# Windowed attention into a two-layer MLP: q/k loads moved to the end of the batch before, eight groups of 256 tokens, buffer fills on POOL and DVE

## The chip, the cores and the metric

One core of one Trainium2 chip. The metric is the device time of the kernel in microseconds (us), the median of several runs. Engines: PE (TensorE, matmuls; its weight loads are listed as PEld), DVE (VectorE), ACT (ScalarE), POOL (GpSimd) and SP (SyncE, which here only issues DMAs, in the order of the program). Every engine works through its own queue in order and waits for others by semaphores.

## The reference

q, k and v are 8 batches x 8 heads x 576 tokens x 64, fp32. Attention is limited to a window of 32 tokens on either side. Its output, with the heads side by side, is a matrix of 4608 tokens x 512, and goes through two matrices with a leaky ReLU between them.

```python
scores = scale * np.matmul(q, k.transpose(0, 1, 3, 2))
mask = np.abs(pos[:, None] - pos[None, :]) <= window
scores = np.where(mask, scores, -1000000000.0)
attn = np.exp(scores - max); attn = attn / sum(attn)
x = np.matmul(attn, v)                      # 4608 x 512 in all
h = x @ w_in                                # 512 x 2048
out = np.maximum(0.01 * h, h) @ w_out       # 2048 x 512
```

## The kernel before

**Attention** goes in steps of one pair of heads each. Batches 0 and 1 (`BY_DMA = 2`, steps 0 to 15, "old" steps) are done in half batches of 288 tokens; their queries and keys are transposed on PE (`transposes`, L321). Batches 2 to 7 (steps 16 to 71) are done in blocks of 64 tokens, four blocks and one pair of heads to a step; their queries and keys are transposed by DMA (`transpose_dma`, L302). A step of the new kind is:
- `score_blocks` (L370): four matmuls of 128 columns (L377), an exponential on ACT (L382), a product with the band mask on POOL (L384). It runs two steps ahead.
- `product_blocks` (L388): eight matmuls of 64 columns (L395) that give the weighted values and, through columns of ones beside the values, the sums; two ACT copies (L402, L403), a reciprocal (L404) and two products into `xT` (L408) on DVE.

**The MLP** goes in groups of tokens (`GROUPS`, L490). For each of 16 tiles f of the hidden layer `h_tile` issues four matmuls (L500) into one of four PSUM buffers `mm`, and ACT applies the leaky ReLU into `gT` (L514). Then `o_tile` (L537) makes 128 tokens of output from 16 matmuls of 512 columns (L549), ACT copies them (L554), and SP stores them (L555, three buffers `o_sb`). The groups are four of 288 tokens (batches 0 and 1), four of 256, four of 512 and one of 384.

**Order.** Up to group 1 the order is written out by hand (L625 to L748). From there a plan of "h" and "o" units with a cost each (L753 to L762) runs on a clock, and each attention step has a due time (L768 to L779) such that every group has its tokens 5 us ahead; `spend` (L783) puts a step before the first unit whose clock has reached its due time. `step` (L585) issues the scores of step i + 2, the weighted values of step i, the copies of transposed queries into their padded buffer on DVE (`place_queries`, L314 to L319), then what is due for later batches, and last one `chore`.

**Preparing a batch b.** `base(b)` is its first step: 16, 24, 32 (b = 2 to 4), 40, 52, 60. At step `base(b) + p - 7` POOL casts q and k of pair p (`cast_qk`, L285), and SP issues their two transposes (L305), which wait for the casts. Three steps later DVE places the queries, one step after that (`base(b) + p - 3`) POOL casts v (`cast_vw`, L298 to L300). q and k of one pair index have one buffer (`qf`, `kf`), v too (`vbuf`), so a load of batch b + 1 waits for the cast of batch b. Before the change, `load_qk(b + 1, p)` (L82, L87) stands in the step of `cast_qk(b, p)`, behind its transposes; batch 3 is loaded in steps 13 to 16, batch 2 by `second_pair` (L723). `load_v_pairs` (L109, five DMAs for two pairs) of the next batch stands at step `base(b) + p - 2` with p = 1 and 3.

**Fills.** The new steps need two sets of buffers `qz` (queries, zero in the other head's rows), `kz` and `vw` (values, with columns of ones). They share memory with the buffers of batches 0 and 1 and are filled while these are worked on, by generators that do one fill each time they are asked: `clear_q` (L228; ACT at L233, others at L236), `set_ones` (L239; ACT at L244, others at L249, each with two small POOL fills), `clear_k` (L254). The list `chores` is worked off by `chore()`, the list `more` by `chore(more)`. Before the change, ACT fills six parts of `qz` at tiles f = 4 to 9 of group 0 while DVE fills six others at f = 5, 7, ... 15; at f = 8 to 15 of group 1 DVE clears the last four parts and sets the first two ones; ACT sets the other six ones at steps 14, 15 and 17 to 20. POOL also clears `kbd[1]` and `vbd[1]` of batch 1 (L719, L746).

Of the kernel before, what the change touches and what calls it, by code (L numbers as in the profile page):

```python
# [16 lines left out]
def kernel(  # L17
# [15 lines left out]
    nc = tc.nc  # L33

    B, H, S, D = q.shape
# [5 lines left out]
    NPAIR = H // 2  # L41
# [25 lines left out]
    BY_DMA = 2  # L67

    def load_qk(b, p, behind=None):

        for into, src, name in ((qf, q, "qf"), (kf, k, "kf")):
            t = fload.tile([96, 2, RUN * D], FP32, name=f"{name}{p}")
            if behind is not None:
                behind.memset(t[0:1, 0, 0:1], 0.0)
                behind = None
            heads = src[b, 2 * p:2 * p + 2]
            if b < BY_DMA:
                nc.sync.dma_start(out=t, in_=heads.rearrange("a (p c) d -> p a (c d)", c=RUN))  # L80
            elif into is qf:
                nc.sync.dma_start(  # L82
                    out=t.rearrange("p a (g e) -> p a g e", g=3),
                    in_=heads.rearrange("a (g p c) d -> p a g (c d)", g=3, c=2),
                )
            else:
                nc.sync.dma_start(  # L87
                    out=t.rearrange("p a (c d) -> p a c d", d=D),
                    in_=heads.rearrange("a (c p) d -> p a c d", p=96),
                )  # L90
            into[b, p] = t
# [96 lines left out]
    for lo in (0, 64):  # L188
# [3 lines left out]
            base=0, channel_multiplier=-1, pattern=[[1, 2], [0, 3], [2, 64]],  # L192
# [3 lines left out]
            base=2 * W, channel_multiplier=1, pattern=[[-1, 2], [0, 3], [-2, 64]],  # L196
# [31 lines left out]
    def clear_q(i, pairs, eng):  # L228
        for p in pairs:
            for a in range(2):  # L230
                r = slice(64 * (1 - a), 64 * (1 - a) + 64)
                if eng is nc.scalar:
                    eng.activation(  # L233
                        out=qz[i][r, p, a], in_=zero[r].to_broadcast([64, S]), func=AF.Copy)
                else:
                    eng.memset(qz[i][r, p, a], 0.0)  # L236
                yield

    def set_ones(i, pairs, eng):  # L239

        for p in pairs:
            to = vw[i][:, p, :, 1]
            if eng is nc.scalar:
                eng.activation(  # L244
                    out=to, in_=one.to_broadcast([128, NB * D]).rearrange("p (m d) -> p m d", d=D),
                    func=AF.Copy,
                )
            else:
                eng.memset(to, 1.0)  # L249
            nc.gpsimd.memset(vw[i][0:W, p, 0, 1], 0.0)  # L250
            nc.gpsimd.memset(vw[i][128 - W:128, p, NB - 1, 1], 0.0)
            yield

    def clear_k(i):  # L254
        nc.gpsimd.memset(kz[i][:, :, 0:W], 0.0)
        nc.gpsimd.memset(kz[i][:, :, KPAD - W:], 0.0)
        yield
# [21 lines left out]
    def cast_qk(b, p, q_eng=None):  # L279
        for eng, src, dst in ((q_eng or nc.gpsimd, qf, qb), (nc.gpsimd, kf, kb)):  # L280
            to, tok = dst[:, p], src[b, p].rearrange("p a (c d) -> p c a d", d=D)
            if eng is nc.scalar:
                eng.activation(out=to, in_=tok, func=AF.Copy)
            else:
                eng.tensor_copy(out=to, in_=tok)  # L285
# [25 lines left out]
    def base(b):  # L311
        return OLD + NPAIR * (NB * (b - BY_DMA) // 4)

    def place_queries():  # L314
        while landing and landing[0][0] <= state["done"]:
            _, b, p, t = landing.pop(0)
            for a in range(2):
                r = slice(64 * a, 64 * a + 64)
                nc.vector.tensor_copy(out=qz[b % 2][r, p, a], in_=t[r])  # L319
# [30 lines left out]
    def place_keys():  # L350

        while unplaced:
            b, p, kT = unplaced.pop(0)
            for a in range(2):
                r = slice(64 * a, 64 * a + 64)
                nc.vector.tensor_copy(  # L356
                    out=kbd[b % 2][r, p, :, r], in_=kT[r].rearrange("p (n j) -> p n j", j=64))
# [52 lines left out]
    def score(i):  # L410
        if i >= OLD:
            return score_blocks(i)
        b, hf, p = where(i)
        by_c = qT[b][:, p].rearrange("p (c i) -> p c i", c=2)
        for n_, blocks in enumerate(WIN[hf]):
            for blk, i0, n in blocks:
                nc.tensor.matmul(  # L417
                    ps_v[:, n_, :, i0:i0 + n], kbd[b % 2][:, p, blk],
                    by_c[:, :, hf * EVEN + i0:hf * EVEN + i0 + n], start=True, stop=True,
                )  # L420
        e = attn.tile([128, 2 * HALF], BF16, name="e")
        nc.scalar.activation(out=e, in_=ps[:, P0:P0 + 2 * HALF], func=AF.Exp, scale=scale)  # L422
        pr = prob[:, i % NPROB]
        nc.gpsimd.tensor_mul(  # L424
            pr.rearrange("p n c i -> p (n c i)"), e, mask[hf].rearrange("p n c i -> p (n c i)"),
        )
        probs[i] = [pr, None, None]

    def join(i):


        pr = probs[i][0].rearrange("p n c i -> p n (c i)")
        both = joined.tile([128, HALF], BF16, name="both")
        nc.vector.tensor_add(both, pr[:, 0], pr[:, 1])
        probs[i][1] = both
# [42 lines left out]
    def weighted(i):  # L478
        if i >= OLD:
            return product_blocks(i)  # L480
        if probs[i][2] is None:
            sums(i)
        product(i)
        scaled(i)
# [5 lines left out]
    GROUPS = [(HALF * g, HALF) for g in range(2 * BY_DMA)]  # L490
    t0, new = 0, NTOK - BY_DMA * S
    while t0 < new:
        n = 256 if t0 < 1024 else min(512, new - t0)
        GROUPS.append((t0 % NEW_RING, n))
        t0 += n

# [71 lines left out]
    JOINED = 12  # L568
    state = {"done": 0}

    qk_due, v_due, v_next = {}, {}, {}
    for b in range(BY_DMA, B):
        for p in range(NPAIR):
            qk_due.setdefault(base(b) + p - 7, []).append((b, p))
            v_due.setdefault(base(b) + p - 3, []).append((b, p))
            if b + 1 < B and p % 2 == 1:
                v_next.setdefault(base(b) + p - 2, []).append((b + 1, p - 1))

    chores = []

    def chore(from_=chores):
        while from_ and next(from_[0], "end") == "end":
            from_.pop(0)

    def step():  # L585
        i = state["done"]
        if JOINED - 1 <= i < OLD - 1:
            join(i + 1)
        if i < NC - 2:
            score(i + 2)  # L590
        weighted(i)
        place_keys()
        place_queries()
        for b, p in qk_due.get(i, ()):
            cast_qk(b, p)
            transpose_dma(b, p)
        for b, p in v_due.get(i, ()):
            cast_vw(b, p)
        for b, p in v_next.get(i, ()):
            load_v_pairs(b, p)  # L600
        for b, p in qk_due.get(i, ()):
            if BY_DMA < b < B - 1:
                load_qk(b + 1, p)
        if 12 < i <= 12 + NPAIR:
            load_qk(BY_DMA + 1, i - 13)
        if i == OLD - 2:
            chores.append(set_ones(0, (2, 3), nc.scalar))
        if i == OLD:
            chores.extend([clear_k(1), set_ones(1, range(NPAIR), nc.scalar)])
        if OLD - 6 <= i < OLD - 3:  # L610
            next(band_parts)
        chore()
        state["done"] += 1
# [92 lines left out]
            score(i + 3)  # L706
        state["done"] += 1

    chores.extend([clear_q(1, (0, 1), nc.scalar), clear_q(0, (2,), nc.scalar)])
    more = [clear_q(1, (2, 3), nc.vector), clear_q(0, (3,), nc.vector)]  # L710
    for f in range(4, FFC):
        h_tile(0, f)
        chore()
        if f % 2 == 1:
            chore(from_=more)
        if f in (5, 9, 13):
            second_half()
        if f % 2 == 1:
            nc.gpsimd.memset((kbd if f < 12 else vbd)[1][:, (f - 4) // 2 % 4], 0.0)  # L719
    second = transposes(1)  # L720
    chores.extend([clear_q(0, (0, 1), nc.vector), clear_k(0), set_ones(0, (0, 1), nc.vector)])

    def second_pair(p):  # L723
        next(second)
# [14 lines left out]
    for f in range(4, FFC):  # L739
        h_tile(1, f)  # L740
        if f >= 8:
            chore()
        if f in (7, 11):
            second_pair((f - 7) // 4)
        if f in (7, 9):
            nc.gpsimd.memset(vbd[1][:, (f - 3) // 2], 0.0)  # L746
        if f == 13:
            score(8)  # L748
# [90 lines left out]
```

## Time and profile before

| | us |
|---|---|
| median of 3 runs | 323.22 (323.21 to 324.9) |
| the profiled execution | 323.49 |
| its span, first to last instruction | 321.8 |
| PE busy | 300.6 |
| DVE busy | 226.5 |
| ACT busy | 221.8 |
| POOL busy | 199.5 |
| granted TensorE clock, mean | 0.998 |

A group line of the profile has the source line, engine, operation, tiles written and read, shape and count, then the busy time, the mean length of one, and the engine's idle time just before them with what ended it. A timeline row has start, length, engine, line, operation, shape and count, and in brackets the idle time before it. A waits row has who waited for whom, the total in us, how often, and the longest. L numbers are lines of the kernel. "SPq" are DMA issues of SP.

The time falls into a start of some 30 us, in which loads and the first attention steps fill PE only partly, a middle up to 170 us in which all engines and the DMA queue are well used, and an end in which PE has no gap.

### The profile page before, as it was taken

To read this page: it belongs to the slowest core of one execution; us is meant where nothing else is said; L and a number is where in the kernel's file an instruction comes from. 1 tells how busy PE (TensorE), PEld (TensorE's weight loads), DVE (VectorE), ACT (ScalarE), POOL (GpSimd) and SP (SyncE) were. 2 spreads that over 40 slices of the span, in tenths; PEclk is the share of its full clock that TensorE was granted. 3 is DMA by queue.
4 is the path that set the end of the run, shared out by engine and by line. 5 is a ranking of instruction groups with operands and counts; after the bars stand their busy time and mean duration, and the time that the engine had idled before them with its cause. 6 is when DMAs were issued, how large, how long until landed. Compare 5 with 4: busy or idle time off the path is not lost.

```text
span 321.8 us, 6551 instructions
## 1 busy us (share of the span) xinstructions
PE 300.6 (93%) x2377; PEld 182.0 (57%) x2377; DVE 226.5 (70%) x295; ACT 221.8 (69%) x478; POOL 199.5 (62%) x262
## 2 busy tenths in 40 slices
PE   2778898999999989999999999999999999999995
PEld 1556674576665756767675555555555555544643
DVE  5688867879867978899799866677678766753000
ACT  7687797666795857778686975697569747852731
POOL 7888944899888867787777326677767722110000
PEclk9999999999999999999999999999999999999999
DMA  8999999977999999999989903995492011001001
GB/s 186 227 194 226 268 240 209 220 190 158 209 250 178 199 218 210 201 200 218 179 174 215 206 2 83 221 229 116 101 198 56 2 65 66 2 33 67 34 32 66
DMA packets 122416, 49.45 MB, mean 154 GB/s; under 512 B 96656, under 2 KB 117904, under 8 KB 122384
## 3 DMA queue, kind: packets, MB, share of 16 engines
q1 hardware_dynamic: 118160, 44.84, 69.4%
q0 software_dynamic: 4224, 4.19, 7.9%
q8 instruction: 18, 0.29, 0.4%
q14 instruction: 14, 0.11, 0.1%
HBM read 36.70 MB, written 9.44 MB: 143 GB/s over the span
## 4 chain that ended last, share of the span: by engine, by line
PE 79%; ACT 8%; DVE 7%; issue 2%; DMA 2%; POOL 1%; ACTq 0%; POOLq 0%; DVEq 0%
PE mm L549 35%; PE mm L500 32%; PE ps L377 4%; ACT gT L514 2%; PE s L395 2%; DMA kT<-qb 2%; PE x L395 2%; DVE set L319 2%; DVE r L451 1%; PE ps L417 1%; DVE r L404 1%; PE x L462 1%; ACT e L422 1%; DVE set L356 1%; POOL prob L424 1%
## 5 line engine op out<-in xcount | busy, mean ns | idle before, releaser
L500 PE MATMUL mm<-xT,w_in_bf 128*128 128x288 bf16 (+3 forms) x832 | 135.6, 313 | 2.5 <-ACT gT L514 2.4
L549 PE MATMUL mm<-w_out_bf,gT 128*128 128x512 bf16 (+2 forms) x592 | 131.8, 373 | 0.0
L404 DVE RECIPROCAL r<-r 128x256 f32<-128x256 f32 (+1 forms) x56 | 95.0, 1696 | 41.0 <-ACT r L403 40.4
L384 POOL TENSOR_TENSOR prob<-e,band 128x512 bf16<-128x512 bf16 (+1 forms) x56 | 62.6, 1118 | 68.1 <-ACT e L382 64.2
L500 PEld LDWEIGHTS <-w_in_bf 128*128 128x128 bf16 x832 | 79.0, 98 | 44.8 <-issue 4.2
L514 ACT ACTIVATE gT<-mm 128x288 bf16<-128x288 f32 (+3 forms) x208 | 87.9, 469 | 15.0 <-PE mm L500 11.8
L549 PEld LDWEIGHTS <-gT 128*128 128x128 bf16 x592 | 55.1, 98 | 57.7
L382 ACT ACTIVATE e<-ps 128x512 bf16<-128x512 f32 (+1 forms) x56 | 32.5, 580 | 43.5 <-PE ps L377 41.3
L554 ACT ACTIVATE o_sb<-mm 128x512 f32<-128x512 f32 (+2 forms) x37 | 21.7, 585 | 24.2 <-PE mm L549 23.6
L451 DVE RECIPROCAL r<-s 128x288 f32<-128x288 f32 x16 | 31.3, 1954 | 4.8 <-PE s L446 3.9
L285 POOL CAST kb<-kf 96x768 bf16<-96x768 f32 x32 | 27.1, 847 | 5.0 <-DMA kf<-in_k_dram 4.8
L319 DVE COPY set<-kT 64x576 bf16<-64x576 bf16 x48 | 25.3, 527 | 2.7 <-DMA kT<-qb 1.7
L408 DVE TENSOR_TENSOR xT<-s,r 64x256 bf16<-64x256 f32 (+1 forms) x56 | 23.1, 413 | 3.3
L408 DVE TENSOR_TENSOR xT<-x,r 64x256 bf16<-64x256 f32 (+1 forms) x56 | 23.1, 413 | 3.3
L424 POOL TENSOR_TENSOR prob<-e,mask 128x576 bf16<-128x576 bf16 x16 | 20.4, 1273 | 7.7 <-ACT e L422 6.7
L377 PEld LDWEIGHTS <-set 128*128 128x128 bf16 x216 | 16.9, 98 | 13.5 <-DMA set<-kb 1.6
L377 PE MATMUL ps<-set 128*128 128x128 bf16 x216 | 22.0, 219 | 2.1 <-DVE set L319 2.0
L285 POOL CAST qb<-qf 96x768 bf16<-96x768 f32 x24 | 19.7, 819 | 0.0
L298 POOL CAST set<-vbuf 128x640 bf16<-128x640 f32 x24 | 17.8, 742 | 0.7 <-DMA vbuf<-in_v_dram 0.7
L395 PEld LDWEIGHTS <-set 128*128 128x128 bf16 x432 | 18.0, 98 | 0.5
L299 POOL CAST set<-vbuf 64x512 bf16<-64x512 f32 x24 | 14.6, 610 | 1.5
L300 POOL CAST set<-vbuf 64x512 bf16<-64x512 f32 x24 | 14.6, 610 | 1.1
(74 smaller groups left out, 220.7 us busy)
## 6 DMA issues: line engine op xcount, KB each, us to landing
qf<-in_q_dram SPq DMA_DIRECT2D x32, 288.0 KB, 4.6
kf<-in_k_dram SPq DMA_DIRECT2D x32, 288.0 KB, 5.4
out_dram<-o_sb SPq DMA_DIRECT2D x35, 256.0 KB, 3.6
vbuf<-in_v_dram SPq DMA_DIRECT2D x36, 128.0 KB, 3.5
vbuf<-in_v_dram SPq DMA_DIRECT2D x16, 144.0 KB, 6.2
vbuf<-in_v_dram SPq DMA_DIRECT2D x24, 96.0 KB, 3.4
w_in_bf<-in_moe_w_in_dram POOLq DMA_DIRECT2D x4, 512.0 KB, 7.9
w_out_bf<-in_moe_w_out_dram POOLq DMA_DIRECT2D x4, 512.0 KB, 15.6
```

Of the source, the lines that this page charges most:

```text
L285: eng.tensor_copy(out=to, in_=tok)
L319: nc.vector.tensor_copy(out=qz[b % 2][r, p, a], in_=t[r])
L377: nc.tensor.matmul(sc[:, :, w], kz[b % 2][:, p, 64 * m:64 * m + 128], tok[:, :, m // 3, :, at:at + 32], start=True, stop=True,)
L382: nc.scalar.activation(out=e[:, 0:n], in_=ps[:, lo:lo + n], func=AF.Exp, scale=scale)
L384: nc.gpsimd.tensor_mul(pr, e[:, 0:n], band.rearrange("p w c i -> p (w c i)")[:, 0:n])
L395: nc.tensor.matmul(x[:, a, w], vw[b % 2][:, p, m, a:a + 2].rearrange("p n d -> p (n d)"), pr[:, a, w], start=True, stop=True,)
L404: nc.vector.reciprocal(r[:, 0:n], r[:, 0:n])
L408: nc.vector.tensor_mul(xT[rows, p, t0:t0 + n], x[rows, a], r[rows, 0:n])
L451: nc.vector.reciprocal(r, s)
L500: nc.tensor.matmul(h[:, 0:n], w_in_bf[:, c, ts(f, 128)], xT[:, c, t0:t0 + n], start=(c == 0), stop=(c == DMC - 1),)
L514: nc.scalar.activation(out=to, in_=h, func=AF.Prelu, alpha=0.01)
L549: nc.tensor.matmul(o[:, lo:hi], gT[:, f, t0:t0 + 128], w_out_bf[:, f, lo:hi], start=(f == 0), stop=(f == FFC - 1),)
```

## The change

- The loading of q and k in `step` by `qk_due` goes. A table `qk_next` puts `load_qk(b + 1, p)` at step `base(b) + p - 4`, three steps later than before and behind all four pairs of transposes of batch b. For batch 3 that is steps 12 to 15, one earlier than before.
- `load_v_pairs` of the next batch moves one step earlier, into the step of the last v cast that it waits for.
- The groups of 256 tokens go from four to eight; two of 512 go.
- The ones of set 0 (pairs 2, 3) and set 1 are set by DVE, no longer by ACT, in the same steps.
- In group 0 ACT fills nothing. DVE does six fills there as before, but of the parts that ACT had filled. The six parts that DVE had filled there are filled by POOL at f = 8 to 13 of group 1.

```diff
-        n = 256 if t0 < 1024 else min(512, new - t0)
+        n = 256 if t0 < 2048 else min(512, new - t0)
...
-    qk_due, v_due, v_next = {}, {}, {}
+    qk_due, qk_next, v_due, v_next = {}, {}, {}, {}
...
+            if b + 1 < B:
+                qk_next.setdefault(base(b) + p - 4, []).append((b + 1, p))
             if b + 1 < B and p % 2 == 1:
-                v_next.setdefault(base(b) + p - 2, []).append((b + 1, p - 1))
+                v_next.setdefault(base(b) + p - 3, []).append((b + 1, p - 1))
...
-        for b, p in qk_due.get(i, ()):
-            if BY_DMA < b < B - 1:
-                load_qk(b + 1, p)
-        if 12 < i <= 12 + NPAIR:
-            load_qk(BY_DMA + 1, i - 13)
+        for b, p in qk_next.get(i, ()):
+            load_qk(b, p)
         if i == OLD - 2:
-            chores.append(set_ones(0, (2, 3), nc.scalar))
+            chores.append(set_ones(0, (2, 3), nc.vector))
         if i == OLD:
-            chores.extend([clear_k(1), set_ones(1, range(NPAIR), nc.scalar)])
+            chores.extend([clear_k(1), set_ones(1, range(NPAIR), nc.vector)])
...
-    chores.extend([clear_q(1, (0, 1), nc.scalar), clear_q(0, (2,), nc.scalar)])
-    more = [clear_q(1, (2, 3), nc.vector), clear_q(0, (3,), nc.vector)]
+    more = [clear_q(1, (0, 1), nc.vector), clear_q(0, (2,), nc.vector)]
     for f in range(4, FFC):
         h_tile(0, f)
-        chore()
         if f % 2 == 1:
             chore(from_=more)
...
+    more = [clear_q(1, (2, 3), nc.gpsimd), clear_q(0, (3,), nc.gpsimd)]
...
         h_tile(1, f)
         if f >= 8:
             chore()
+            chore(more)
```

## The prediction

> **What bounds the kernel now.** I read the busy shares first, then the 40 slices, then the PE rows of the waits and of the timeline.
>
> ```profile
> PE 300.6 (93%) x2377; PEld 182.0 (57%) x2377; DVE 226.5 (70%) x295; ACT 221.8 (69%) x478; POOL 199.5 (62%) x262
> PE   2778898999999989999999999999999999999995
> PE mm L500 <- ACT gT L514: 2.4, 7, 0.5
> PE ps L377 <- DVE set L319: 2.0, 2, 1.3
> ```
>
> PE is the bound, and it is full from about 170 us to the end. So only PE time lost before 170 us can be won. A matmul's drawn end is modelled, so I count lost time from start to start. Runs without waits give the pitch of each shape: 216 ns for 512 columns, 122 for 288, 109 for 256. What the PE timeline has beyond these pitches is lost: 9.3 us before 30 us, 2.9 from 30 to 48.7, 1.5 to 80, 1.9 to 110, 2.4 to 140, 1.1 to 170, then nothing. The first 9.3 us lie ahead of every line that the diff touches. About 10 us are within reach, 3% of the time.
>
> ```profile
> 34.52 0.65 PE L500 MATMUL mm<-xT,w_in_bf 128*128 128x288 bf16 x4 [0.49 <-ACT gT L514]
> 34.49 0.68 ACT L233 ACTIVATE set<-zero 64x576 bf16<-64x576 bf16 x1
> 90.39 2.12 PE L500 MATMUL mm<-xT,w_in_bf 128*128 128x288 bf16 x16
> 92.89 1.14 PE L500 MATMUL mm<-xT,w_in_bf 128*128 128x288 bf16 x8 [0.37 <-ACT gT L514]
> 91.86 0.68 ACT L244 ACTIVATE set<-one 128x576 bf16<-128x576 bf16 x1
> 117.64 0.33 PE L377 MATMUL ps<-set 128*128 128x128 bf16 x3 [1.33 <-DVE set L319]
> 116.97 0.62 DVE L319 COPY set<-kT 64x576 bf16<-64x576 bf16 x2 [1.75 <-DMA kT<-qb]
> ```
>
> Columns: start, length, engine and line, [idle before, and what ended it]. Between two gT activations ACT fills a buffer for 0.68 us, and PE waits for gT. From 90.39, 16 x 122 ns end at 92.34, but PE goes on at 92.89: 0.55 lost. At 116.10 one score matmul starts, the next at 117.64: 1.48 lost, because DVE placed the queries late, because their transpose landed late.
>
> **Part 1, zero fills of the first two stretches.** Six ACT fills of 0.68 us (L233, 28.5 to 35.2) go. PE lost 0.62 + 0.51 + 0.65 = 1.78 us there. DVE does six zero fills of 0.30 us there as before, and they are late next:
>
> ```profile
> 32.06 1.95 DVE L451 RECIPROCAL r<-s 128x288 f32<-128x288 f32 x1
> 34.01 0.69 DVE L236 MEMSET set<- 64x288 uint32 x2
> 35.45 0.46 DVE L476 TENSOR_TENSOR xT<-x,r 128x288 bf16<-128x288 f32 x1 [0.74 <-PE x L462]
> ```
>
> DVE runs without a break from 26.23 to 34.70; its only slack is this 0.74. The product xT of step 7 (37.99) hangs on that chain, and group 1 needs it. So of 1.78 at most 0.74 comes through.
>
> Then POOL gets six fills at f = 8 to 13 of group 1. POOL fills cost 0.52 us for 512 elements and 1.05 for 1152, by which 576 take 0.58, together 3.5 us. They stand behind the cast at 42.68, among two 1.05 us fills:
>
> ```profile
> 43.91 2.00 DVE L285 CAST qb<-qf 96x768 bf16<-96x768 f32 x1
> 48.31 0.56 DVE L285 CAST qb<-qf 96x768 bf16<-96x768 f32 x1
> 43.45 2.05 POOL L746 MEMSET set<- 128x1152 bf16 x2
> 42.68 0.82 POOL L285 CAST kb<-kf 96x768 bf16<-96x768 f32 x1 [2.56 <-DMA kf<-in_k_dram]
> ```
>
> The same DVE cast takes 0.56 us beside an idle POOL and 2.00 beside two POOL fills; it ends 0.4 after the second. The Trainium skill (SBUF — State Buffer, Who interferes with whom) says that such a DVE cast and a POOL instruction need one port pair, which the first to issue holds for its whole length. The row agrees for one fill but not for two, since the cast stood there before the second. By that rule alone the cast would lose at most 1.05 us.
>
> POOL is idle 2.56, 1.01 and 1.93 us around the new fills, but the second gap waits for a load (kf, landing at 46.5), so not all of it is usable. The key cast at 46.50 moves to some 48 or 49, the first prob product behind it from 49.96 to about 50.9. PE needs that product near 52. Best case: the DVE cast, due 0.74 earlier at 43.2, gets in right after the cast at 42.68, ends at 44.0 in place of 45.9, and the 0.60 us that PE lost at 47.5 (score, L417, waiting for L356) goes as well: +1.3. Worst case: it waits for all 2 x 1.05 + 4 x 0.58 = 4.4 us of fills: -2.3, below. I take **+0.5**, nearer to the good end, since a cast on POOL did let a DVE cast in at 38.3.
>
> **Part 2, ones of the second buffers (L244 to L249).** ACT loses six times 0.68 us. PE lost 0.54 + 0.55 in group 3, each right behind such a fill. The group before, without a fill in it (and with lighter steps on ACT), lost nothing. **+1.0**. DVE gains six times 0.54 (the L249 row). At steps 17 to 19 DVE idles 1.2 to 1.7 us before each reciprocal, which covers it; at 14 and 15 it is dense, but PE has the wider spacing of part 4. At step 20 it is not covered, which part 3 counts.
>
> **Part 3, the loads.** Line 603 issued two DMAs (0.57 + 0.51 us of SP) right behind each pair of transposes. Now they come three steps later, behind all four pairs. The v loads (five DMAs, 3.2 to 4.9 us of SP) move one step earlier, ahead of the next batch's transposes.
>
> ```profile
> 109.28 0.57 SPq L82 DMA_DIRECT2D qf<-in_q_dram  x1
> 109.90 0.50 SPq L87 DMA_DIRECT2D kf<-in_k_dram  x1
> 110.50 0.54 SPq L555 DMA_DIRECT2D out_dram<-o_sb  x1
> 111.14 1.32 SPq L305 DMA_TRANSPOSE kT<-qb  x1
> ```
>
> POOL had cast this pair by 101.9; SP reached its transpose at 111.14, and it landed at 116.94. Without three pairs of loads (3.3 us) and the v loads at 96.12 (3.9) ahead of it, it lands before DVE is free at 115.2. Lost around there: 0.80 (108.66) + 0.23 + 1.48 = 2.51. What is late next is DVE: reciprocal 1.75, two products 0.86, two copies 1.5, and once 0.54 for the ones. The step spacing helps: from step 20 to step 23 PE has 10.0 us of work before, 10.9 after. The first loss becomes 0.80 + 0.54 - 0.88 = 0.46, the others nothing: **+2.0** (from 0.9, if DVE gains nothing from the spacing, to 2.5). The next batch lost 0.16 + 0.25 in the same way: **+0.2**.
>
> New waits: the v load now waits on SP for POOL's three casts of its own step (1.9 us). Behind it stand output stores, which have three buffers, the next q/k loads, needed five or more steps (18 us) later, and transposes that need a later POOL cast anyway. Batch 3's loads go one step earlier, ahead of batch 2's last v load (some 1.1 us of SP): its cast waited 0.70 at 82.05 already, but the prob product behind it is ready 4.4 us ahead of its use. Both cost nothing unless several such delays add up.
>
> **Part 4, eight groups of 256.** On PE, two matmuls of 256 in place of one of 512: 2 x 109 - 216 = 2 ns, times 128 = 0.26 us. The Trainium skill (TensorE: Matmul & The Clock Gate, Back-to-back issue gap) has two prices: N/2.4 + 2.5 ns, which the rows match, and a sustained 81 ns at 128 against 131 at 512. From the latter I estimate 98 at 256, thus 65 ns lost per pair, 8.3 us; the rows 109 and 216 speak against it.
>
> ACT pays more: 64 x 391 ns for 32 x 596, 5.9 us. Per tile that is 391 of PE's 436 ns, and each step adds 1.36 us to ACT but 0.45 to PE.
>
> ```profile
> 125.00 1.91 PE L500 MATMUL mm<-xT,w_in_bf 128*128 128x256 bf16 x16
> 127.08 1.47 PE L500 MATMUL mm<-xT,w_in_bf 128*128 128x256 bf16 x12 [0.17 <-ACT gT L514]
> ```
>
> From 125.00, 16 x 109 end at 126.74; 0.34 lost. The four present 256 groups lose to ACT 0.26, 0.47, 0.26 and 0.46 us: 0.34 where a step comes with the first tiles, 0.13 where it comes in the middle. The 512 groups lose nothing. Counting where the planner puts steps 22 to 54, the eight lose about 3.1: **-1.6**, with the matmuls **-1.9**. The planner (lines 751 to 779) sets steps 12 to 39 every 3.06 us before and every 3.21 after, up to step 55: that is the wider spacing.
>
> **Sum.** +0.5 + 1.0 + 2.0 + 0.2 - 1.9 = +1.8. The profiled execution took 323.49 (span 321.8, 1.7 around it), which becomes 321.7; it stands 0.27 above the median of 323.22. For the median: **321.4 us**, 0.6% less. About 0.5%, or 1.6 us, is what a measurement can tell from no change.
>
> **Rivals.**
> - *No change: DVE takes ACT's place.* The ones at step 20 keep the query chain as late as it was (part 3 gives 0.9), part 1 gives nothing: 0 + 1.0 + 0.9 + 0.1 - 1.9 = 0.1, so 323.1. For it: DVE is dense in both stretches. Against: the wider spacing. 0.25.
> - *The loads do not do what they are moved for:* the v loads, now earlier, hold SP in place of the q/k loads, and the last transpose lands as late as now. Part 3 loses 1.5: 322.9. Against: POOL, not SP, would then set the issue. 0.08.
> - *Slower: the POOL fills lock DVE out.* Place: the cast at 43.9. If it waits out six fills in a row, it ends at 48.3, not 45.9; the score at 48.34 then starts near 50.7. Part 1 is -2.3 and the sum -1.0: 324.2. It decides if that cast issues after the first fill has begun (about 43.5); DVE is due at 43.2, so it is close. 0.12.
> - *Slower: ACT bounds the 256 groups.* Without the cover of the four PSUM buffers, a group with three steps lacks 16 x 0.391 + 3 x 1.36 - 16 x 0.436 - 3 x 0.45 = 2.0 us; four more groups cost 8: +3.7 - 0.3 - 8.0 = -4.6, so 327.8. It decides if ACT comes late into a group. The present groups, at most 0.47, speak against it. 0.05.
>
> **Numbers.** My forecast's case, 319.4 to 322.3, has 0.50. Faster by over 0.5%: most of it and the gains beyond, 0.48. Within 0.5%: the first two rivals, the forecast's upper end and most of the third, 0.40. Slower: the fourth and the bad end of the third, 0.12. Range 319.4 to 324.3: all but the fourth rival, an even better part 1, and sums of several delays.
>
> **What would show it.** No PE wait for gT from 31 to 35 and in group 3; the copies L319 of the last pair not waiting for DMA; the DVE cast near 43.5 shorter than 2.0; eight 256 groups each losing 0.2 to 0.5; nothing lost after 170. Wrong if a 256 group loses over 0.6, if the score behind the new POOL fills starts after 49, or if SP holds a transpose behind v loads.

## The result, and the profile after

The changed kernel takes **321.36 us** (median of 9 runs, 320.87 to 322.44); the kernel before, run beside it on the same chip, 323.67 (9 runs, 323.18 to 326.24). The ratio is **0.9917**, 95% interval 0.9892 to 0.9942: 0.8% faster. The profiled execution after took 321.36 with a span of 319.7; that of before 323.49 with 321.8. Of the 90 runs of the kernel before that stand beside the experiments below, 40 show a granted TensorE clock of 0.990 to 0.995 and are 2.4 to 2.8 us longer in the median than the others of the same group, while none of the changed kernel's 16 runs lies under 0.999. First the page of the changed kernel, its busy shares and PE's 40 slices:

```profile
PE 300.4 (94%) x2505; PEld 194.6 (61%) x2505; DVE 229.0 (72%) x301; ACT 217.3 (68%) x498; POOL 203.9 (64%) x268
PE   2678898999999999999999999999999999999995
```

PE's busy time is what it was; the slice with an 8 in the middle of before (112.6 to 120.6 us, the scores of batch 3) has become a 9. ACT lost work (six fills and six ones less, more evictions), DVE and POOL have taken it over. Next the PE rows of the waits, the first one from before, the others from after:

```profile
PE s L446 <- POOL prob L424: 2.5, 3, 1.7
PE s L446 <- POOL prob L424: 3.9, 4, 1.7
PE mm L500 <- ACT gT L514: 0.9, 5, 0.2
PE mm L500 <- DVE xT L476: 0.5, 1, 0.5
```

The row of the scores (L377 waiting for L319), 2.0 us before, is gone. The waits for gT fell from 2.4 to 0.9, though there are eight groups of 256 now. New are waits for DVE in the first groups, for xT (0.5) and for a reciprocal (0.4); the waits for POOL's products grew from 2.5 to 3.9. The lost time, counted from start to start of the matmuls beyond the pitch of their shape, as in the prediction, and sorted by place (us):

| place | before | after | won | forecast |
|---|---|---|---|---|
| up to 66 us (part 1) | 4.33 | 3.55 | 0.8 | 0.5 |
| steps 13 and 16, weighted values | 0.08 | 0.50 | -0.4 | 0 |
| group 3, waiting for gT (part 2) | 1.07 | 0 | 1.1 | 1.0 |
| scores of batch 3, steps 23 to 25 (part 3) | 2.53 | 0.11 | 2.4 | 2.0 |
| scores of batch 4 | 0.41 | 0.19 | 0.2 | 0.2 |
| groups of 256, waiting for ACT (part 4) | 1.45 | 3.13 | -1.7 | -1.6 |
| matmul time itself (part 4) | | | -0.3 | -0.3 |
| sum | | | **2.1** | **1.8** |

PE's last matmul ends at 318.45 us before and at 316.34 after, 2.1 earlier, so the table holds the whole difference of the two profiled executions. The lines of the changed kernel's timeline behind its larger entries:

```profile
37.72 2.90 PE L500 MATMUL mm<-xT,w_in_bf 128*128 128x288 bf16 x20 [0.50 <-DVE xT L476]
43.20 1.36 DVE L285 CAST qb<-qf 96x768 bf16<-96x768 f32 x1
50.93 1.26 POOL L424 TENSOR_TENSOR prob<-e,mask 128x576 bf16<-128x576 bf16 x1
52.25 0.41 PE L446 MATMUL s<-prob,ones_bd 128*128 128x288 bf16 x2 [1.48 <-POOL prob L424]
82.56 0.39 PE L395 MATMUL x<-prob,set 128*128 128x64 bf16 x8 [0.34 <-DVE xT L476]
107.13 1.24 SPq L305 DMA_TRANSPOSE kT<-qb  x1
115.26 1.26 DVE L319 COPY set<-kT 64x576 bf16<-64x576 bf16 x2
```

With ACT's fills gone PE waits for DVE instead: xT of step 7 comes at 37.28 in place of 37.99, 0.71 earlier, and PE waits for it. The query cast on DVE takes 1.36 us, not 2.00. The six POOL fills put the mask product at 50.93, and PE waits 1.48 for it. In step 16 PE waits for xT of step 15. SP issues the last query transpose of batch 3 at 107.13 (before 111.14); it lands at 109.67 (before 116.94), and its copy on DVE, at 115.26, has no idle time in brackets: it waits for nothing any more.

### The profile page after: what moved, and what is told of

Read it like the earlier page. It is cut to its first block, busy times and chain, and to the rows that moved or that the text cites. A ratio compares the mean times of both kernels' runs of the same rounds, so it can differ in the third digit from the quotient of the medians.

```text
span 319.7 us, 6829 instructions
## 1 busy us (share of the span) xinstructions
PE 300.4 (94%) x2505; PEld 194.6 (61%) x2505; DVE 229.0 (72%) x301; ACT 217.3 (68%) x498; POOL 203.9 (64%) x268
## 4 chain that ended last, share of the span: by engine, by line
PE 74%; DVE 8%; ACT 5%; POOL 5%; DMA 4%; issue 3%; SPq 0%; POOLq 0%; ACTq 0%; DVEq 0%
PE mm L549 34%; PE mm L500 30%; DMA kf<-in_k_dram 4%; DVE r L451 4%; PE ps L377 3%; PE s L395 2%; PE x L395 2%; POOL prob L424 1%; POOL set L236 1%; ACT e L382 1%; ACT gT L514 1%; DVE set L319 1%; PE s L446 1%; DVE xT L476 1%; PE ps L417 1%
## 5 line engine op out<-in xcount | busy, mean ns | idle before, releaser
L500 PE MATMUL mm<-xT,w_in_bf 128*128 128x256 bf16 (+3 forms) x960 | 135.8, 294 | 1.5 <-ACT gT L514 0.9
L500 PEld LDWEIGHTS <-w_in_bf 128*128 128x128 bf16 x960 | 91.5, 98 | 33.7 <-issue 2.7
L514 ACT ACTIVATE gT<-mm 128x256 bf16<-128x256 f32 (+3 forms) x240 | 91.3, 432 | 16.5 <-PE mm L500 12.0
L319 DVE COPY set<-kT 64x576 bf16<-64x576 bf16 x48 | 25.2, 524 | 1.4 <-DMA kT<-qb 0.5
L377 PEld LDWEIGHTS <-set 128*128 128x128 bf16 x216 | 16.8, 98 | 9.6
L377 PE MATMUL ps<-set 128*128 128x128 bf16 x216 | 21.5, 219 | 0.0
```

What stands on the lines that cost most here:

```text
L377: nc.tensor.matmul(sc[:, :, w], kz[b % 2][:, p, 64 * m:64 * m + 128], tok[:, :, m // 3, :, at:at + 32], start=True, stop=True,)
L500: nc.tensor.matmul(h[:, 0:n], w_in_bf[:, c, ts(f, 128)], xT[:, c, t0:t0 + n], start=(c == 0), stop=(c == DMC - 1),)
L514: nc.scalar.activation(out=to, in_=h, func=AF.Prelu, alpha=0.01)
```

## The experiments

All kernels were timed beside the kernel before. That one scatters: its median was 323.67 on the chip of the result and 325.1 to 325.4 on the chips of the experiments (single runs from 322.66 to 329.5), while the changed kernel gave 321.36 and 321.39. So I compare the experiments by their own medians and by the lost time in their profiles, and give the ratio to before with its interval; the ratio also holds the clock of before's runs. The changed kernel was timed on the chip of the result and on one of the experiments' three, so some of the differences of medians below are between chips; the kernel before has medians within 0.3 us of each other on these three. What the longer runs of before lose, no profile shows: the one taken is near their lower end. Diffs are against the changed kernel or against the one before, as the sentence ahead says.

### One part alone

**Loads alone** (the kernel before, with the q, k and v loads moved):

```diff
+                qk_next.setdefault(base(b) + p - 4, []).append((b + 1, p))
-                v_next.setdefault(base(b) + p - 2, []).append((b + 1, p - 1))
+                v_next.setdefault(base(b) + p - 3, []).append((b + 1, p - 1))
...
-        for b, p in qk_due.get(i, ()):
...
+        for b, p in qk_next.get(i, ()):
+            load_qk(b, p)
```

> The kernel before with the loads moved and nothing else (four groups, ACT fills). Theory, two limits lie one behind the other at steps 20 to 27, the landing of the transposes and the query chain on DVE, and the loads remove only the first: of the 2.5 us that PE loses there 0.8 to 1.5 stay, no DVE wait for DMA above 0.5, -1.0 to -1.7 us. Rival, the landing was the whole cause: under 0.4 us stays, -2.2. Rival, the loads alone give nothing since DVE is as late without them: -0.3 or less.

Measured: 322.49 us, ratio 0.9913 (0.9877 to 0.9948). The scores of batch 3 lose 1.08 us (0.25 + 0.83) in place of 2.53, as expected. But PE loses 1.5 us in a new place, step 18, to POOL, which has waited 6.60 us for batch 2's last v load:

```profile
90.81 0.39 PE L395 MATMUL x<-prob,set 128*128 128x64 bf16 x8 [1.34 <-POOL prob L384]
116.56 0.33 PE L377 MATMUL ps<-set 128*128 128x128 bf16 x3 [0.67 <-DVE set L319]
```

The first row is what the loads cost, the second what they left. The loads do what they are moved for, and take something back at a spot that the prediction costed at nothing (below).

**Groups alone** (the kernel before, eight groups of 256):

```diff
-        n = 256 if t0 < 1024 else min(512, new - t0)
+        n = 256 if t0 < 2048 else min(512, new - t0)
```

> The kernel before (323.67) with eight groups of 256 and nothing else. Theory A: 1.9 us lost to matmul pitch and ACT, but the spacing gives steps 20 to 27 about 1.7 us more, and the last transpose of batch 3 then lands in time although its place on SP is the old one: 2.4 of the 2.5 us lost there come back; sum -0.5, 323.2. Theory B, the loads have to move for that: the first score wait goes (0.8), the wait for the transpose (1.48) stays: +1.1, 324.8. Both: PE still waits for gT behind L244 in group 3.

Measured: 323.57 us, ratio 0.9951 (0.9919 to 0.9983); profiled 323.74, so 0.25 above that of before. The 256 groups lose 3.09 (1.45 before), the scores of batch 3 lose 1.38 (2.53 before) and those of batch 4 0.18 (0.41): the wider spacing gives back 1.4 of the 1.6 us. At the scores of batch 3 this lies between the two theories: 1.15 of the 2.5 us came back. DVE still waits for the transposes:

```profile
113.49 0.95 DVE L319 COPY set<-kT 64x576 bf16<-64x576 bf16 x2 [1.94 <-DMA kT<-qb]
```

**Fills alone** (the kernel before, with the fills and ones of the change):

```diff
-            chores.append(set_ones(0, (2, 3), nc.scalar))
+            chores.append(set_ones(0, (2, 3), nc.vector))
...
-            chores.extend([clear_k(1), set_ones(1, range(NPAIR), nc.scalar)])
+            chores.extend([clear_k(1), set_ones(1, range(NPAIR), nc.vector)])
...
+            chore(more)
```

> The kernel before with the fills moved and nothing else (old loads, four groups). Theory: 0.8 us won up to 66 us, 1.07 in group 3; at the scores of steps 23 to 27 DVE carries the ones of step 20 too and the transposes still land late: 2.5 us lost there become 3.2 to 3.8. Sum -0.6 to -1.2 us, 322.5 to 323 where the kernel before takes 323.7. Rival: the fills are worth their full 1.9 us, 321.8, since PE's wait at the scores is set by the landing alone and hides the ones.

Measured: 324.01 us, ratio 0.9979 (0.9948 to 1.0011): no gain that can be told. Group 3 loses nothing and 0.6 is won up to 66 us, but the scores of batch 3 now lose 4.69 us, more than expected. Its timeline, PE and DVE:

```profile
109.30 0.33 PE L377 MATMUL ps<-set 128*128 128x128 bf16 x3 [2.92 <-DVE set L319]
107.73 1.52 DVE L319 COPY set<-kT 64x576 bf16<-64x576 bf16 x2 [2.08 <-DMA kT<-qb]
```

What is won early arrives at the scores as waiting: PE comes there sooner, the transposes do not (SP issues the last query transpose at 111.95, before at 111.14). The outcome is that of the prediction's rival "DVE takes ACT's place", but by another way: the copies of the first and the third of these scores wait for the transfer (2.08 and 1.64 us), so here the landing comes last, and not DVE's ones.

### One part undone

**Loads back in their old steps** (the changed kernel with the opposite of the first diff):

```diff
-                qk_next.setdefault(base(b) + p - 4, []).append((b + 1, p))
-                v_next.setdefault(base(b) + p - 3, []).append((b + 1, p - 1))
+                v_next.setdefault(base(b) + p - 2, []).append((b + 1, p - 1))
```

> The changed kernel (321.4) with the loads of q, k and v in their old steps; fills and eight groups as changed. Theory A, the spacing alone keeps the queries in time: PE waits for L319 under 0.5 us around step 25 to 27, 321.6. Theory B, the loads are needed: SP reaches the last transpose of batch 3 some 9 us after its cast, as before, and PE loses 1 to 1.5 us there: 322.6 to 322.9. Both: POOL's wait for batch 2's last v load (3.7 us in the changed kernel) is back at 0.7.

Measured: 323.3 us, ratio 0.9941 (0.9909 to 0.9974). The scores of batch 3 lose 3.03 us, batch 4 0.84. Three copies of queries wait for their transposes again, 2.00, 1.59 and 1.04 us; the first two:

```profile
108.26 1.04 DVE L319 COPY set<-kT 64x576 bf16<-64x576 bf16 x2 [2.00 <-DMA kT<-qb]
113.63 0.62 DVE L319 COPY set<-kT 64x576 bf16<-64x576 bf16 x2 [1.59 <-DMA kT<-qb]
```

At step 18 PE loses nothing, and POOL waits 1.29 us for the v load. Undoing the loads' move costs 1.9 us of the 321.4. Of the gain 0.6% is left beside the kernel before on the same chip, 0.1% beside the 323.67 of the first chip, and the profiled execution (324.51, 1.2 above its median) is 1.0 longer than that of before.

**Four groups of 256 again** (the changed kernel, one line):

```diff
-        n = 256 if t0 < 2048 else min(512, new - t0)
+        n = 256 if t0 < 1024 else min(512, new - t0)
```

> The changed kernel (321.4) with four groups of 256 again, all else as changed. Theory A, the groups cost PE time but their wider step spacing pays part of it: back come 0.26 us of matmul pitch and about 1.7 us of waits for ACT in four groups; lost is the spacing at steps 20 to 27, where the query chain on DVE, now with the ones in it, makes PE wait 0.80 + 0.54 us at the first score and 0.2 at the second (0.1 in all in the changed kernel), less the 0.5 us that PE loses at step 16 to the tighter place of that step. Sum about -0.9: 320.5. Theory B, the spacing is worth nothing, since the loads alone cured the late queries: 319.0 to 319.5, and no PE wait for L319 above 0.3. Theory C, the eight groups are themselves the gain: 322.5 or more.

Measured: 322.12 us, ratio 0.9928 (0.9891 to 0.9965), so none of the expected times; three of its twelve runs have a granted clock of 0.995, and the other nine a median of 321.74. The groups' ACT waits fall back to 1.45, but the scores of batch 3 lose 2.67 us (1.41 + 0.84 + 0.42) with the loads moved. The prediction's rule for the first of them (0.80 + 0.54 - 0.88 for the spacing) gives 1.34 without the spacing, and 1.41 was measured. The agreement proves little: with the loads alone moved, and no ones on DVE, this first wait is 0.01 and not 0.80, though PE comes there late by its wait at step 18. Here DVE is late by its own work: the copy below has no wait for a transfer in brackets, and PE waits behind it:

```profile
109.93 1.70 DVE L319 COPY set<-kT 64x576 bf16<-64x576 bf16 x2
111.69 0.33 PE L377 MATMUL ps<-set 128*128 128x128 bf16 x3 [0.68 <-DVE set L319]
```

So the eight groups cost 1.9 us on ACT and PE and give about 2.5 back at the scores: beside the other parts they about pay for themselves.

**Fills back on ACT and DVE** (the changed kernel with the opposite of the fills' diff):

```diff
-            chores.append(set_ones(0, (2, 3), nc.vector))
+            chores.append(set_ones(0, (2, 3), nc.scalar))
...
+    chores.extend([clear_q(1, (0, 1), nc.scalar), clear_q(0, (2,), nc.scalar)])
+    more = [clear_q(1, (2, 3), nc.vector), clear_q(0, (3,), nc.vector)]
```

> The changed kernel (321.4) with all fills on the engines of before; loads and eight groups as changed. Theory A, ACT's fills cost PE time in two places: 0.85 us up to 53 us and 1.07 in group 3 come back as losses, 0.5 at step 16 (where DVE's ones made PE wait for xT) is won: +1.4, 322.8. Rival: DVE and POOL only took the loss over and the fills are worth nothing, 321.4, the PE waits for gT being matched by waits for DVE and POOL that go.

Measured: 322.41 us, ratio 0.9925 (0.9893 to 0.9957). 1.06 us are lost in group 3, as expected, and none at the scores of batch 3, where DVE has no ones to set and PE comes later by what it lost ahead; which of the two does it was not separated. The fills' move is worth 1.0 in the medians. Its profiled execution is 1.2 above its median and lost 5.41 us up to 66; POOL's key cast waited 3.65 us for its load there (2.56 before), and the query cast on DVE stood beside that cast (43.76 to 44.58) and two fills:

```profile
43.90 3.09 DVE L285 CAST qb<-qf 96x768 bf16<-96x768 f32 x1
44.53 2.05 POOL L745 MEMSET set<- 128x1152 bf16 x2
```

The scores of batch 3 in all eight combinations (loads, groups and fills as before or as after), lost us:

| | old loads | new loads |
|---|---|---|
| four groups, old fills | 2.53 (before) | 1.08 |
| eight groups, old fills | 1.38 | 0 |
| four groups, new fills | 4.69 | 2.67 |
| eight groups, new fills | 3.03 | 0.11 (after) |

One place, three causes in series: when the transposes land, how dense DVE is, and how far the steps lie apart. The new fills (ones on DVE, and PE earlier) cost 1.6 to 2.2 us here unless both other parts are there; then 0.1. Each cell is one profile; a second one of the changed kernel has 0.46 in place of 0.11.

### The step that was costed at nothing

**The changed kernel once more**, with no edit, to see what another execution shows:

> The changed kernel itself, beside the next three on one chip. 0.7 to 0.9% below the kernel before. In its trace PE loses 3.1 to 3.2 us from 30 to 53 us, 0.5 at step 16, 0.1 to 0.2 at the scores of steps 23 to 25, and 3.1 in all to ACT in the eight groups of 256.

Measured: 321.39 us (7 runs, 320.95 to 322.95), ratio 0.9906 (0.9872 to 0.9939). The profiled execution is the longest of these, 322.95, 1.6 longer than the first. PE lost 0.85 at step 16, 1.34 at step 18 and 0.46 at the scores of batch 3. Its timeline:

```profile
87.81 0.72 POOL L298 CAST set<-vbuf 128x640 bf16<-128x640 f32 x1 [6.16 <-DMA vbuf<-in_v_dram]
91.53 0.39 PE L395 MATMUL x<-prob,set 128*128 128x64 bf16 x8 [1.18 <-POOL prob L384]
```

POOL waits 6.16 us for batch 2's last v load, its band product behind the casts comes late, and PE waits for that. The same cast in the first execution of the changed kernel:

```profile
85.36 0.72 POOL L298 CAST set<-vbuf 128x640 bf16<-128x640 f32 x1 [3.69 <-DMA vbuf<-in_v_dram]
```

and in the kernel before:

```profile
82.05 0.72 POOL L298 CAST set<-vbuf 128x640 bf16<-128x640 f32 x1 [0.70 <-DMA vbuf<-in_v_dram]
```

In the first execution the product behind it was still 1.2 us ahead of its use, before the change 4.4. So some executions pay here and others do not. In the seven profiles with batch 3's loads moved ahead of this v load POOL waits 3.4 to 7.0 us for it, and PE loses at step 18 in the three with over 6 us (1.34, 1.50 and 2.15); in the four with the loads in their old steps POOL waits 0.7 to 2.3, and PE loses nothing there.

**Ones one step later** (the changed kernel; aimed at the 0.50 of step 16, where DVE sets ones ahead of step 15's reciprocal):

```diff
-        if i == OLD - 2:
+        if i == OLD - 1:
             chores.append(set_ones(0, (2, 3), nc.vector))
...
+        if i == OLD:
+            chore()
```

> The changed kernel with the ones of set 0 set by DVE one step later (steps 15 and 16, not 14 and 15). Theory, the fill ahead of the reciprocal of step 15 is what makes PE wait 0.5 us at step 16: that wait falls below 0.1, nothing else moves, -0.5 us. Rival, the place of step 16, closer to step 15 by the new spacing, is the cause: 0.5 us stays.

Measured: 321.59 us, ratio 0.99 (0.9864 to 0.9937). The wait is gone, but the scores of batches 3 and 4 lose 0.34 + 0.70 where the changed kernel loses 0.11 + 0.19, and the time is the same.

**Three moves** (the above; DVE's six fills of group 0 moved to the free steps 8 to 11; and two POOL fills of `vbd` moved ahead of the new ones):

```diff
+        if i in (8, 9, OLD):
+            chore()
...
+        if f in (4, 5):
+            nc.gpsimd.memset(vbd[1][:, f - 2], 0.0)
...
-        if f in (7, 9):
-            nc.gpsimd.memset(vbd[1][:, (f - 3) // 2], 0.0)
```

> A version meant to beat the changed kernel, with three moves: ones of set 0 one step later, the two 1152-element POOL fills of batch 1 at f = 4 and 5 of group 1 (POOL is idle 3.2 us there) instead of f = 7 and 9, and the six DVE fills of group 0 in steps 8 to 11. Theory, each removes a wait named in the trace: 0.5 at step 16, 0.4 of the 1.6 at 50.6 (then ACT's casts of v are late), 1.2 of the 1.5 that the DVE chain costs between 33 and 38 us: -2.0 us, 0.6% below the changed kernel. Rival, the loads of batch 1 arrive late (keys of pair 2 land at 42.3, pair 3 at 45.8) and set the pace from 40 to 50 us: only 0.5 to 1.0 us comes through.

Measured: 322.42 us, ratio 0.9936 (0.9904 to 0.9967). Up to 66 us only 1.98 us are lost in place of 3.55, as expected. At step 18 it is gone again (2.15, behind a wait of 6.96 us of POOL for the v load), and the scores lose 0.97:

```profile
90.38 0.39 PE L395 MATMUL x<-prob,set 128*128 128x64 bf16 x8 [1.99 <-POOL prob L384]
```

**The v load one step earlier** (the changed kernel; batch 2's second v load behind step 11, ahead of batch 3's q and k loads):

```diff
-            if i in (10, 12):
-                clear_vf(i - 10)
-                load_v_pairs(BY_DMA, i - 10)
+            if i in (10, 11):
+                clear_vf(2 * (i - 10))
+                load_v_pairs(BY_DMA, 2 * (i - 10))
```

> The changed kernel with the v load of batch 2's second pair of pairs behind step 11, not 12, so that batch 3's q and k loads, now one step earlier, no longer stand ahead of it. Theory, that order is a wait that the change adds: POOL's cast of that v waited 0.7 us for DMA before and 3.7 and 6.2 us in two profiles of the changed kernel, and PE lost 0 and 1.3 us behind it at step 18. Here POOL waits under 1.5 us, PE loses nothing at step 18 in any profile, and the median falls by 0.3 to 0.8 us below the changed kernel's 321.4. Rival, the DMA engines are full there whatever the order: POOL still waits 3 us or more, or the transposes of batch 2's last pair, now behind that load, make DVE wait instead; no gain.

Measured: 322.45 us, ratio 0.9913 (0.9886 to 0.9941). POOL's cast waits for no load any more and step 18 loses nothing: it was the order of the loads. But the median is worse than the changed kernel's (the intervals of the ratios overlap), by neither expectation's reason. PE loses 1.45 us at steps 13 to 15, and 0.65 at step 16 (0.50 in the changed kernel), to DVE:

```profile
75.32 0.41 PE L462 MATMUL x<-prob,set 128*128 128x64 bf16 x5 [0.28 <-DVE xT L476]
70.86 1.97 DVE L434 TENSOR_TENSOR both<-prob 128x288 bf16<-128x288 bf16 x1
70.63 0.80 POOL L218 TENSOR_SCALAR_AFFINE_SELECT band<-band 128x512 bf16<-128x512 bf16 x1
71.40 1.27 POOL L424 TENSOR_TENSOR prob<-e,mask 128x576 bf16<-128x576 bf16 x1
```

A join on DVE (L434, 0.71 us before) takes 1.97, up to the end of two POOL instructions. With the load, the two small POOL fills that clear its edges (0.30 each) left the place between these two.

**The same with two spare POOL fills in that place** (small fills whose result is not used):

```diff
+            if i == 12:
+                nc.gpsimd.memset(spare, 0.0)
+                nc.gpsimd.memset(spare, 0.0)
```

> The kernel with batch 2's second v load behind step 11, and in step 12 two POOL fills of a small spare tile (32 x 192 fp32, some 0.25 us each, their result is not used) between the band's last select and the next product, where the two 0.30 us fills stood before. Theory (a waiting DVE join is let in only between POOL instructions, and long ones back to back keep it out): the join of step 13, 1.97 us without them, takes at most 0.8; the PE waits at steps 13 to 15, 1.45 us without them, fall to 0.5 or less; the time to 321.0 to 321.6. Rival (the joins and copies of steps 12 to 14 are simply too many for DVE, and the long join only shows it): the waits stay over 1.0 us and the time at 322.0 to 322.6. Either way POOL's wait for the v load before step 18's casts stays gone.

Measured: 321.86 us, ratio 0.9896 (0.9857 to 0.9935). The join takes 0.71 again, as the theory has it; it ends 0.14 after the select, while the spare fill is under way:

```profile
71.32 0.71 DVE L435 TENSOR_TENSOR both<-prob 128x288 bf16<-128x288 bf16 x1
71.84 0.25 POOL L795 MEMSET spare<- 32x192 f32 x1
```

PE loses 0.67 us there in place of 1.45; the rest stands behind the next join, 1.25 us beside a POOL product. Step 16 loses 0.65 as without the spare fills. The time lies 0.3 us above the expected range and 0.6 below that without the spare fills (the intervals overlap), and still not below the changed kernel's. So what follows the select on POOL sets the length of this join, and the rest of DVE's density there is not cured by it.

**All four moves together** (the three moves and the v load):

> The version with three moves and the same earlier v load. Theory: the three moves lost their gain to the wait at step 18 (2.15 us there in its profile); without it 322.4 falls to 320.2 or so, 1.2 us below the changed kernel, and PE loses about 2.0 us up to 66 us, nothing at step 18, 0.5 to 1.0 at the scores of steps 23 to 25. Rival: what is won early is lost again at these scores, since PE arrives there earlier and DVE does not: 321.0 to 321.5.

Measured: 321.43 us (320.82 to 322.14), ratio 0.9893 (0.9852 to 0.9934). It beats the kernel before, but cannot be told from the changed kernel (321.36, 321.39): of 1.6 us won early, 1.56 are lost at steps 13 to 15, 0.70 at batch 4's scores, where the changed kernel loses 0.19, and 0.21 at batch 5's. That is the rival's time, but not its place: the scores of steps 23 to 25 lose nothing.

## Why the prediction was right

The forecast was 321.4 us and 0.6% less; 321.36 and 0.8% less were measured, and each term of the sum has its sign and nearly its size. That the two times lie within 0.1 us is luck: the kernel before took 323.67 beside the changed one, not the 323.22 that the sum starts from, so the gain is 2.3 us and not 1.8, and among the terms errors of +0.3, +0.4 and -0.4 cancel in part.

- **Part 1 (+0.5, measured 0.8).** Right in its mechanism: of 1.78 us on ACT only 0.71 came through, the bound read from DVE's chain being 0.74. The cast on DVE got in after one POOL fill (1.36 us), and the mask product started at 50.93 where 50.9 was worked out. So behind the fills the 0.61 at the score (L417) is gone, but 1.64 are lost at the mask product, where 1.11 were lost to a cast of v on ACT (L291). That 0.61 moves with the landing of the key load ahead of the fills: where the fills are those of before, the key cast on POOL starts at 41.81, 42.50, 42.68 and 43.76 in four profiles, and 0, 0.44, 0.61 and 1.69 us are lost. In eight profiles with the new fills it starts at 41.74 to 42.45, the cast on DVE takes 0.89 to 1.58, and at most 0.18 is lost. The rival "POOL fills lock DVE out" had its condition met, a cast that issues after the first fill has begun (43.20 against 43.09), but needed the cast to wait for all six, and it waited for one. It is not far off, though: with a later load the cast takes 3.09 (fills back).
- **Part 2 (+1.0, measured 1.1).** Right; undoing the fills brings 1.06 back. The ones on DVE were called covered at steps 17 to 19 and, through the wider spacing, at 14 and 15. They were not at step 14: its 0.54 us stands at 79.50 ahead of step 15's reciprocal, and PE loses 0.50 in step 16. With the ones a step later that wait is gone.
- **Part 3 (+2.0, measured 2.4).** The transposes land in time and DVE is late next, as said. The first wait was to stay at 0.46; the profiled execution has none there and 0.11 at the third score, the second execution 0.33 + 0.13 at the second and the third. The reckoning came out where the spacing was taken away (1.34 against 1.41), with the doubt named there. But a sign of being wrong did show, without a price: SP held transposes behind the v loads. POOL had cast batch 3's first pair by 94.11, and its transpose was issued at 98.58, behind the row below; the other transposes follow back to back, so SP and not POOL still set the issue of the last one (cast by 102.50, issued at 107.13). That the transposes behind the v loads "need a later POOL cast anyway" was wrong, and the rival that the v loads hold SP was right in its mechanism and wrong in its effect, since the last copy comes 5.6 us after the landing.

```profile
92.57 5.38 SPq L116 DMA_DIRECT2D vbuf<-in_v_dram  x5
```

- **Part 4 (-1.9, measured 1.68 + 0.26).** The eight groups lose 3.13 against "about 3.1", each 0.13 to 0.59 (forecast 0.2 to 0.5, wrong over 0.6). The rival "ACT bounds the 256 groups" needed 2.0 per group. By the pitches PE's matmul time grew by 0.26 us. The 65 ns per pair estimated from the Trainium skill's sustained figures (TensorE: Matmul & The Clock Gate, Back-to-back issue gap) would have been 8.3 us; the traces do not agree with it.
- **Costed at nothing, and not nothing:** batch 3's q and k loads ahead of batch 2's last v load. The cover of 4.4 us that I read is right for one execution of before, but falls to 1.2 in one of after, and in another one PE loses 1.34. The step that failed is "some 1.1 us of SP": the cast that waits for this load starts 3.3 us later than before in one execution (85.36 against 82.05) and 5.8 in the other (87.81).
- **"Nothing lost after 170"** was wrong by its own part 4: of the 3.13 us that the groups of 256 lose, 1.79 lie behind 170 us, up to 225.
- **Not priced at all:** what each part is worth by itself. The sum treated the parts as terms. At the scores they are not: the fills alone cost there what they win (4.69 lost against 2.53), the loads alone win 1.45, all three 2.4. In medians, undoing the loads costs 1.9 us, the fills 1.0, the groups 0.7 (0.4 without the three runs at the lower clock). So the total is right also because all three were made together.

Open stays why the kernel before scatters by up to 7 us on one chip and the changed kernel by 2. The lower granted clock named with the result goes with part of it; in the one profile of before the clock is 1.00 up to PE's last matmul, so where it falls, and why more often in that kernel, is not shown. The late v load accounts for 1.34 of the 1.6 us by which the second profiled execution of the changed kernel is longer than the first.

## What to carry to other kernels

Where an early gain arrives at a later wait it is lost, so causes that act in series on one place (a transfer, a dense engine, the spacing of the steps) are priced together, in the order in which they become the last. A load that is moved forward in a queue that issues in order takes its time from the loads it overtakes (here 3.3 and 5.8 us for 1.1 us of issue): count their cover, and in more than one execution if the loads' landing varies. A fill is free only on an engine that idles at that very place.

## What the runs showed of the hardware

- A DVE instruction that is ready while POOL works can be kept out for more than one POOL instruction: the query cast takes 0.56 us alone, 1.36 behind one fill, 2.00 behind two in a row, and 3.09 beside a cast and two fills. The join (two inputs in SBUF), drawn as started during a select on POOL, takes 0.71 when small fills follow the select, and 1.97 when a product does. The Trainium skill says that POOL and a DVE instruction that uses both port pairs, as a cast can, share one pair, and that whoever issues first gets it for the whole instruction (SBUF — State Buffer, Who interferes with whom). The traces agree for one POOL instruction; in the 2.00 and the 3.09 a POOL instruction got in that began after DVE's had been drawn as started, and so it did in the join's 1.97. Behind the fill of the 1.36 POOL is idle for 0.06 us (44.14 to 44.20), between the two of the 2.00 not at all; but the join of 1.25 got in without such a gap, and what decides was not tried.
- Two small fills between the select and the product let the join through. The same section of the Trainium skill says that a DVE instruction with two inputs in SBUF contends with a POOL instruction that reads SBUF, not with one that only writes it. The runs agree: 0.71 beside fills, 1.25 and 1.97 beside products and selects.
- POOL pays too: the fill of 576 elements ahead of which the cast got in is drawn with 0.87 us, the next one with 0.57.
